# Windowed attention and a gated feed-forward layer: the product with w_in rewritten as seven block products, with chunks of 512 tokens

## The chip, the cores and the metric

One core of one Trainium2 chip runs the whole program. The metric is the device time of one execution in microseconds (us); lower is better. The core has five engines that run side by side and wait for each other through semaphores: TensorE (PE, matrix products into PSUM), VectorE (DVE), ScalarE (ACT), GpSimd (POOL) and SyncE (SP, which issues DMAs). Operands lie on chip in SBUF; products land in PSUM, of which the kernel uses eight banks of 128 x 512 float32.

## What is computed

```python
# q, k, v: (8 batches, 8 heads, 576 tokens, 64), float32; q and k are scaled by 8
scores = q @ k.T / 8 + slope[h] * -(i - j)            # ALiBi bias, slope[h] = 2 ** -(h + 1)
scores = where((i - j >= 0) & (i - j < 128), scores, -1e9)
attn = softmax(scores)
x = (attn @ v) as (4608 tokens, 512)                   # heads side by side
h = x @ w_in                                           # w_in: 512 x 2048, w_out: 2048 x 512
g = where(h >= 1, h, where(h <= -1, 0, (h + 1) ** 2 / 4))
out = g @ w_out                                        # 4608 x 512, float32
```

The two weight matrices arrive as 64-bit floats and are converted on the chip.

## The kernel before, in words

The 4608 tokens (the 8 batches behind each other) are cut into 12 chunks of `CH` = 384 tokens, three blocks of 128. Attention looks back 128 tokens, so a block of queries needs its own block of keys and the one in front: a window of 256 keys.

**Precision.** The kernel gives TensorE float32 operands in two forms: as plain float32 (48 written products of L396 stand as 96 instructions in the trace), called the slow form here, or as `F32R` (one instruction each), the fast form. For the fast form a value is split into a high part `a0` (a cast to F32R) and a low part `a1 = a - a0`, and a product is three fast products: `a0 b0 + a0 b1 + a1 b0`. The first `LIGHT` = 2 chunks of attention and the second layer of chunk 0 use the slow form instead, and need no splits.

**Attention**, for each head `m` (8 per chunk): `scores` makes the three windows' products (L246, or L248 and L249), adds the distance table `rel` and takes the row maximum (L252, DVE, 256 wide), exponentiates with a row sum (L254, ACT), and folds the two halves of the window into one 128-wide block while it divides by the sum (L267, DVE). `weights_t` transposes (L276, PE), splits (L286, L287) and cuts the block into the two triangles (L289, L291, POOL). `values` multiplies by v (L317 or L341) and adds up the parts (L342, L343, L345). `prepare_q`, `prepare_k`, `prepare_v` make splits of q, k, v.

**Feed-forward.** `split_x` splits the 512 x 384 block of x (L359, L360). `layer1(c, fc)` makes 128 of the 2048 features for the chunk: 12 products of 384 columns into the single PSUM bank of `ps_h` (L366 to L368), then the nonlinearity in three operations (L375 ACT, L376 and L377 DVE), and the split of g (L384 ACT, L385 POOL). `layer2(c, fc)` adds these features' share of the output into three accumulator banks: 9 products of 512 columns (L399 to L401; L396 in chunk 0). After the last one, L404 scales by 4 and a DMA stores. All split weights stay in SBUF through the run.

**Weights.** `fetch_weights` loads 64-bit pieces, issued on ACT's queue; `float32_of` converts (L115, L116 on ACT; L117, L118, L119 on DVE); `convert_in`, `convert_out` and `split_out` place them and split them (L138, L139, L151, L152).

**Order.** The kernel hands the instructions over in the order of the two interleaved lists at its end: `layer1` of piece i, `layer2` of piece i - `LAG`, and after each some segments of the next chunk's attention, so that attention of chunk c + 1 lies beside the feed-forward of chunk c. A list scheduler with a simulated timeline may move instructions within an engine; the order on each engine is then fixed in the program. PSUM: three accumulators, one bank for h, four for attention (`ps_a`).

Of the kernel before, what the change touches and what calls it, by code (L numbers as in the profile page):

```python
# [14 lines left out]
PSUM = bass.MemoryType.PSUM  # L15


@with_exitstack
def windowed_attention_then_ffn(
# [9 lines left out]

# [5 lines left out]
    DFF = w_in.shape[1]  # L45
# [3 lines left out]
    NFC = DFF // P  # L49
    NQB = 3  # L50
    CH = NQB * P
    NCHUNK = NT // CH
    NP = NCHUNK * NPAIR
    NH = 2 * NP
    CYCLE = 2 * SEQ // CH
    CUT = SEQ - CH
    assert 2 * SEQ == CYCLE * CH and CYCLE == 3 and CUT == P + D
    NEG = -1.0e30

# [3 lines left out]
    wp = ctx.enter_context(tc.tile_pool(name="wp", bufs=1))  # L63
    stg = ctx.enter_context(tc.tile_pool(name="stg", bufs=3))
    ap1 = ctx.enter_context(tc.tile_pool(name="ap1", bufs=1))
    xp1 = ctx.enter_context(tc.tile_pool(name="xp1", bufs=1))
    gp = ctx.enter_context(tc.tile_pool(name="gp", bufs=3))
    ps_acc = ctx.enter_context(tc.tile_pool(name="ps_acc", bufs=NQB, space=PSUM))
    ps_h = ctx.enter_context(tc.tile_pool(name="ps_h", bufs=1, space=PSUM))
    ps_a = ctx.enter_context(tc.tile_pool(name="ps_a", bufs=4, space=PSUM))  # L70

    def bank(name):
        return ps_a.tile([P, 4 * P], F32, name=name, tag="ps_a")

# [3 lines left out]
    quarter = const.tile([P, 1], F32, name="quarter")  # L78
    G.memset(quarter, 0.25)

    loaded = const.tile([P, 1], F32, name="loaded")
    S.activation(loaded, quarter, AF.Exp)
    qscale = const.tile([P, NPAIR], F32, name="qscale")
    for g in range(NPAIR):
        G.memset(qscale[:D, g:g + 1], 4.0 ** g / 4.0)
        G.memset(qscale[D:, g:g + 1], 4.0 ** g / 2.0)

    rel = const.tile([P, 2 * P], F32, name="rel")
    reli = stg.tile([P, 2 * P], I32, name="reli", tag="stg")
    G.iota(reli, pattern=[[1, 2 * P]], base=-P, channel_multiplier=-1)  # L90
    V.tensor_copy(rel, reli)
    G.affine_select(out=rel, in_=rel, pattern=[[1, 2 * P]], base=0, channel_multiplier=-1,
                    compare_op=ALU.is_gt, fill=NEG)
    G.affine_select(out=rel, in_=rel, pattern=[[-1, 2 * P]], base=P, channel_multiplier=1,
                    compare_op=ALU.is_ge, fill=NEG)
# [12 lines left out]

    def float32_of(w, name, out=None):

        low, high = w[..., 0], w[..., 1]
        f = stg.tile([P] + list(w.shape[1:-1]), F32, name=f"f_{name}", tag="stg")
        fi = f.bitcast(I32)

        S.mul(high.bitcast(F32), high.bitcast(F32), 2.0 ** -112)  # L115
        S.activation(low, low.bitcast(U32), AF.Copy, scale=2.0 ** -29)  # L116
        V.tensor_scalar(fi, high, 3, None, ALU.logical_shift_left)  # L117
        V.scalar_tensor_tensor(fi, high, -0x80000000, fi, ALU.bitwise_and, ALU.bitwise_or)  # L118
        V.tensor_tensor(fi if out is None else out.bitcast(I32), fi, low, ALU.add)  # L119
        return f  # L120

    raw = {}

    def fetch_weights(fc):
        w1 = wp.tile([P, NCC, P, 2], I32, name=f"rawi{fc}", tag=f"wi{fc}")
        S.dma_start(w1, wi32[:, 2 * fc * P:2 * (fc + 1) * P].rearrange("(c p) (f w) -> p c f w", p=P, w=2))

        if fc + 1 < NFC:
            w2 = wp.tile([P, DM, 2], I32, name=f"rawo{fc}", tag=f"wo{(fc + 2) % NFC}")
        else:  # L130
            w2 = ap1.tile([P, DM, 2], I32, name=f"rawo{fc}", tag="kl")
        S.dma_start(w2, wo32[fc * P:(fc + 1) * P, :].rearrange("p (f w) -> p f w", w=2))
        raw[fc] = (w1, w2)

    def convert_in(fc):
        f = float32_of(raw[fc][0], f"i{fc}")
        t = wi[fc] = wp.tile([P, 2, NCC, P], F32R, name=f"wi{fc}", tag=f"wi{fc}")
        S.copy(t[:, 0], f)  # L138
        V.tensor_tensor(t[:, 1], f, t[:, 0].bitcast(F32), ALU.subtract)  # L139
# [403 lines left out]
```

## Time and profile before

| what | value |
|---|---|
| times of three executions | 1068.0, 1070.49, 1070.89 us (median 1070.49) |
| profiled execution: span from its first to its last instruction | 1068.8 us |
| share of the span in which PE, DVE, ACT, POOL were busy | 97%, 76%, 58%, 35% |
| TensorE clock granted, mean | 0.980 of full |
| moved between HBM and chip | 69.51 MB |

The profiled execution has no separate time of its own beside the span: 1068.8 us lies inside the three runs' times and 1.7 us under their median. In the profile a line such as `L366 PE MATMUL h<-xh,wi 128*128 128x384 f32 x768` names the kernel line, the engine, the operation, output and inputs by tile name, the shapes, and the count; after it stand the busy time in us, the mean duration of one in ns, the engine's idle time ahead of them and what ended it. A matmul's duration includes its way through the array, so matmuls in a row start closer together than they last.

### The profile page before, as it was taken

To read this page: it belongs to the slowest core of one execution; us is meant where nothing else is said; L and a number is where in the kernel's file an instruction comes from. 1 tells how busy PE (TensorE), PEld (TensorE's weight loads), DVE (VectorE), ACT (ScalarE), POOL (GpSimd) and SP (SyncE) were. 2 spreads that over 40 slices of the span, in tenths; PEclk is the share of its full clock that TensorE was granted. 3 is DMA by queue.
4 is the path that set the end of the run, shared out by engine and by line. 5 is a ranking of instruction groups with operands and counts; after the bars stand their busy time and mean duration, and the time that the engine had idled before them with its cause. 6 is when DMAs were issued, how large, how long until landed. Compare 5 with 4: busy or idle time off the path is not lost.

```text
span 1068.8 us, 16893 instructions
## 1 busy us (share of the span) xinstructions
PE 1041.4 (97%) x5510; PEld 905.7 (85%) x5510; DVE 808.7 (76%) x2281; ACT 619.0 (58%) x1476; POOL 375.6 (35%) x419
## 2 busy tenths in 40 slices
PE   7999999999999999999999999999999999999998
PEld 5566668998999988998988998899899889899996
DVE  3889999879778788779887788877787897863322
ACT  4687767557557556557565555655565655742322
POOL 1121104343443343344443343344334444333221
PEclk7599999999999999999999999999999999999999
DMA  5466412212113112212221311311121221200000
GB/s 179 141 199 198 148 38 67 60 30 82 43 48 94 38 38 78 59 31 70 55 50 43 86 37 47 91 30 38 60 65 38 77 65 40 75 1 1 31 1 29
DMA packets 58904, 69.51 MB, mean 65 GB/s; under 512 B 4032, under 2 KB 44480, under 8 KB 58816
## 3 DMA queue, kind: packets, MB, share of 16 engines
q1 hardware_dynamic: 48064, 51.66, 17.2%
q10 hardware_dynamic: 10752, 16.78, 4.6%
q8 instruction: 43, 0.70, 0.3%
q14 instruction: 45, 0.37, 0.1%
HBM read 58.98 MB, written 9.44 MB: 64 GB/s over the span
## 4 chain that ended last, share of the span: by engine, by line
PE 83%; DVE 7%; ACT 4%; issue 2%; POOL 2%; DMA 1%; ACTq 0%; DVEq 0%; POOLq 0%
PE h L367 11%; PE h L366 11%; PE h L368 11%; PE acc L399 10%; PE acc L400 10%; PE acc L401 10%; PE x L341 5%; PE p L276 3%; PE acc L396 3%; PE x L317 2%; PE s L249 2%; PE s L248 2%; PE s L246 2%; ACT z L254 1%; DVE g L376 1%
## 5 line engine op out<-in xcount | busy, mean ns | idle before, releaser
L385 POOL TENSOR_TENSOR gl<-g,gh 128x384 fp32r<-128x384 f32 x176 | 183.3, 1041 | 414.5 <-ACT gh L384 403.4
L366 PE MATMUL h<-xh,wi 128*128 128x384 f32 x768 | 266.4, 347 | 3.3 <-ACT xh L359 2.8
L367 PE MATMUL h<-xl,wi 128*128 128x384 f32 x768 | 260.7, 339 | 0.4 <-DVE xl L360 0.4
L368 PE MATMUL h<-xh,wi 128*128 128x384 f32 x768 | 259.8, 338 | 0.0
L399 PE MATMUL acc<-wo,gh 128*128 128x512 f32 x528 | 211.8, 401 | 5.7 <-ACT gh L384 5.7
L376 DVE SCALAR_TENSOR_TENSOR g<-sg 128x384 f32<-128x384 f32 x192 | 108.4, 565 | 138.9 <-ACT sg L375 124.5
L400 PE MATMUL acc<-wo,gh 128*128 128x512 f32 x528 | 208.2, 394 | 0.0
L384 ACT CAST gh<-g 128x384 fp32r<-128x384 f32 x176 | 90.3, 513 | 187.8 <-DVE g L377 176.4
L375 ACT ACTIVATE sg<-h,quarter 128x384 f32<-128x384 f32 x192 | 111.1, 579 | 143.1 <-PE h L368 136.7
L401 PE MATMUL acc<-wo,gl 128*128 128x512 f32 x528 | 155.9, 397 | 0.2 <-POOL gl L385 0.2
L366 PEld LDWEIGHTS h<-xh,wi 128*128 128x128 f32 x768 | 144.6, 188 | 13.0 <-ACT xh L359 3.5
L254 ACT ACTIVATE z<-z,nmax 128x256 f32<-128x256 f32 (+2 forms) x288 | 139.1, 485 | 26.3 <-DVE nmax L252 23.2
L367 PEld LDWEIGHTS h<-xl,wi 128*128 128x128 f32 x768 | 144.6, 188 | 8.4 <-issue 2.7
L368 PEld LDWEIGHTS h<-xh,wi 128*128 128x128 f32 x768 | 144.6, 188 | 0.0
L267 DVE CUSTOM_DVE_ANT_0 ep<-z,rc 128x128 f32<-128x128 f32 x256 | 129.8, 548 | 1.3
L252 DVE CUSTOM_DVE_ANT_0 z<-s,rel 128x256 f32<-128x256 f32 (+2 forms) x256 | 94.0, 393 | 41.3 <-PE s L249 36.1
L289 POOL TENSOR_SCALAR_AFFINE_SELECT lu<-lu 128x768 fp32r<-128x768 f32 x80 | 80.7, 1008 | 121.6 <-DVE lu L287 114.1
L399 PEld LDWEIGHTS acc<-wo,gh 128*128 128x128 f32 x528 | 99.4, 188 | 24.8 <-ACT gh L384 8.0
L401 PEld LDWEIGHTS acc<-wo,gl 128*128 128x128 f32 x528 | 97.2, 188 | 19.9 <-POOL gl L385 0.4
L377 DVE SCALAR_TENSOR_TENSOR g<-sg,g 128x384 f32<-128x384 f32 x192 | 111.2, 579 | 3.3
L400 PEld LDWEIGHTS acc<-wo,gh 128*128 128x128 f32 x528 | 99.4, 188 | 16.4
L291 POOL TENSOR_SCALAR_AFFINE_SELECT lu<-lu 128x768 fp32r<-128x768 f32 x80 | 82.6, 1032 | 4.5
(83 smaller groups left out, 1491.5 us busy)
## 6 DMA issues: line engine op xcount, KB each, us to landing
kr<-in_k_dram SPq DMA_DIRECT2D x60, 256.0 KB, 4.1
qr<-in_q_dram SPq DMA_DIRECT2D x48, 192.0 KB, 3.4
out_dram<-o SPq DMA_DIRECT2D x36, 256.0 KB, 3.0
rawi<-in_moe_w_in_dram ACTq DMA_DIRECT2D x16, 512.0 KB, 3.9
rawo<-in_moe_w_out_dram ACTq DMA_DIRECT2D x16, 512.0 KB, 4.8
vn<-in_v_dram SPq DMA_DIRECT2D x32, 256.0 KB, 2.8
kr<-in_k_dram SPq DMA_DIRECT2D x28, 192.0 KB, 3.4
vn<-in_v_dram SPq DMA_DIRECT2D x16, 192.0 KB, 2.5
```

The lines of the kernel that those rows point to most:

```text
L254: S.activation(z[:, i, c0:], z[:, i, c0:], AF.Exp, bias=nmax[:, i:i + 1], scale=-1.0, accum_out=sm[:, i, 0:1])
L267: st["folded"] = V.tensor_tensor_reduce(out=ep[:, i, :], in0=z[:, i, :P], in1=z[:, i, P:], op0=ALU.add, op1=ALU.add, scale=rc[:, i:i + 1], ...
L366: T.matmul(ph, wi[fc][:, 0, cc, :], xh, start=(cc == 0), stop=False)
L367: T.matmul(ph, wi[fc][:, 0, cc, :], xl, start=False, stop=False)
L368: T.matmul(ph, wi[fc][:, 1, cc, :], xh, start=False, stop=(cc == NCC - 1))
L375: first = S.activation(sg, ph, AF.Relu, bias=quarter[:, 0:1], scale=0.25)
L376: V.scalar_tensor_tensor(g, sg, 0.5, sg, ALU.min, ALU.mult)
L377: last = V.scalar_tensor_tensor(g, sg, -0.25, g, ALU.add, ALU.max)
L385: G.tensor_tensor(gl, g, gh.bitcast(F32), ALU.subtract)
L399: T.matmul(a, gh[:, ts], wo[fc][:, 0], start=first, stop=False)
L400: T.matmul(a, gh[:, ts], wo[fc][:, 1], start=False, stop=False)
L401: T.matmul(a, gl[:, ts], wo[fc][:, 0], start=False, stop=last)
```

## The change

The kernel is rewritten around Strassen's algorithm (in Winograd's form) for `x @ w_in`. Chunks now have 2, then eight times 4, then 2 blocks of 128 tokens (`SIZES`): 256, 8 x 512, 256 tokens.

For a chunk of 512 tokens the features are taken in eight groups `g` of 2 x 128 (piece `g` and piece `8 + g`). The weights of a group form a 2 x 2 block matrix (two features pieces x two halves of the 512 inputs), the transposed x another (two halves of inputs x two halves of the tokens). Instead of 8 block products, 7 are made from sums of blocks; each has 6 fast products of 256 columns. Four of the seven accumulate one after another in one PSUM bank (`hA`), with the running sum copied out by ACT after the first three; three use the bank `hB`. DVE adds the copies to form the four blocks of h.

```diff
+PRODUCTS = (("A11", "B11"), ("A12", "B21"), ("S2", "T2"), ("S1", "T1"), ("S4", "B22"), ("S3", "T3"), ("A22", "T4"))
...
+    SIZES = [2] + [4] * 8 + [2]
...
+    def product(o, w, x, start, stop):
+        todo = [(kb, a, b) for kb in range(2) for a, b in ((0, 0), (0, 1), (1, 0))]
+        for n, (kb, a, b) in enumerate(todo):
+            T.matmul(o, w[:, a, kb], x[:, b, kb], start=start and n == 0, stop=stop and n == len(todo) - 1,
+                     skip_group_check=True)
...
+                def prod(n, st=st, g=g):
+                    w, x = PRODUCTS[n]
+                    o = st["A" if n in (0, 2, 3, 4) else "B"]
+                    product(o, use(c, g, w), xs[c, x], start=n in (0, 1, 5), stop=True)
+                    if n in (0, 2, 3):
+                        s = st[n] = fp.tile([P, 2 * P], F32, name=f"s{n}_{c}_{g}", tag=f"s{n}", bufs=1)
+                        S.copy(s, o)
+                    f1, f2 = st["h"]
+                    if n == 1:
+                        V.tensor_tensor(f1[:, :2 * P], o, st[0], ALU.add)
+                    if n == 4:
+                        S.copy(f1[:, 2 * P:], o)
+                        nonlinear(c, g, f1, 4 * P)
+                    if n == 5:
+                        V.tensor_tensor(f2[:, 2 * P:], o, st[3], ALU.add)
+                    if n == 6:
+                        V.tensor_tensor(f2[:, :2 * P], o, st[2], ALU.add)
+                        nonlinear(c, NG + g, f2, 4 * P)
+                    used(c, g, w)
...
+                for n, fill in ((2, 1), (3, 2), (4, 1), (5, 1), (6, 2)):
+                    steps.append([lambda prod=prod, n=n: prod(n), lambda tokens=tokens, n=n: tokens(n)])
+                    steps += [[f] for f in later(fill)]
```

A "fill" is one block of `layer2` (three products of 512 columns for one token block); the fills of a group are those of the group before it. Between product 0 and product 2 lie product 1 and one fill.

The weight operands (`A11`, `A12`, `A22`, and sums `S1` to `S4`) are no longer kept in SBUF. In chunk 1 `build` makes them (the sums on POOL, a cast on ACT, a subtraction on DVE) and stores each split operand, 256 KB, to a scratch in HBM; from chunk 2 on `fetch` streams each one back ahead of every use, ten operands ahead, through a ring of ten buffers. The last chunk uses the plain four blocks. Chunk 0 now makes its first layer in the slow float32 form with unsplit weights.

```diff
+    def build(g, name):
+        f = operand(g, name)
         t = ring.tile([P, 2, 2, P], F32R, name=f"b_{g}_{name}", tag="w")
         S.copy(t[:, 0], f)
         V.tensor_tensor(t[:, 1], f, t[:, 0].bitcast(F32), ALU.subtract)
+        d = scratch[g, name] = dr.tile([P, 4 * P], F32, name=f"d_{g}_{name}", tag=f"d_{g}_{name}")
+        DMA.dma_start(d, t.bitcast(F32).rearrange("p s c f -> p (s c f)"))
+    def fetch(c, g, name):
+        t = ring.tile([P, 2, 2, P], F32R, name=f"w_{c}_{g}_{name}", tag="w")
+        DMA.dma_start(t.bitcast(F32).rearrange("p s c f -> p (s c f)"), scratch[g, name])
+        return t
```

x is combined and split into seven operands instead of four (`combine`, `split_x`: four subtractions more on DVE, three casts and subtractions more).

The nonlinearity becomes clamp, square, maximum, and the factor 4 of the output goes away:

```diff
-        first = S.activation(sg, ph, AF.Relu, bias=quarter[:, 0:1], scale=0.25)
-        V.scalar_tensor_tensor(g, sg, 0.5, sg, ALU.min, ALU.mult)
-        last = V.scalar_tensor_tensor(g, sg, -0.25, g, ALU.add, ALU.max)
+        V.tensor_scalar(m, h, 1.0, -1.0, ALU.min, ALU.max)
+        S.activation(m, m, AF.Square, bias=half[:, 0:1], scale=0.5)
+        V.tensor_tensor(f, h, m, ALU.max)
```

In `scores` each query has exactly 128 keys in its window of 256, one of each pair (j, j + 128). A predicated copy now folds the two halves in PSUM right after the product, so all that follows is 128 wide, and the division by the row sum moves to ACT:

```diff
+        V.copy_predicated(pt[:, :nk, P:], older.unsqueeze(1).broadcast_to([P, nk, P]), pt[:, :nk, :P])
+            V.tensor_tensor_reduce(out=z[:, i], in0=pt[:, n, P:], in1=distances(b0 + i), op0=ALU.add, op1=ALU.min,
+                                   scale=-slope, scalar=3.0e38, accum_out=nmax[:, i:i + 1])
+            S.activation(z[:, i], z[:, i], AF.Exp, bias=nmax[:, i:i + 1], scale=-1.0, accum_out=sm[:, i:i + 1])
...
+                for i in range(nb):
+                    S.activation(z[:, i], z[:, i], AF.Copy, scale=rc[:, i:i + 1])
```

The light chunks' scores use all 128 rows, with zeros in the other head's rows of q. The conversion of the 64-bit weights takes two DVE operations instead of three (the sign comes from a parametric ReLU on ACT), reads through six 512 KB buffers, and its loads are issued on SP's queue together with all others. PSUM: four accumulators, the two banks hA and hB, and two banks for attention instead of four. The host lays v and both weight matrices out so that a load is contiguous.

More of the change, by code (lines that the diff above doesn't have):

```diff
@@ L48, in windowed_attention_then_ffn @@
     NCC = DM // P
[L49 to L57, printed above, removed]
+    NFC = 16
+    NG = NFC // 2
+    SIZES = [2] + [4] * 8 + [2]
+    STARTS = [sum(SIZES[:i]) for i in range(len(SIZES))]
+    NCHUNK = len(SIZES)
+    NH = NCHUNK * H
+    PERIOD = 2 * SEQ // P
+    assert sum(SIZES) * P == NT and 2 * SEQ == PERIOD * P
     NEG = -1.0e30
@@ L122, in windowed_attention_then_ffn @@
[L122 to L133, printed above, removed]
@@ L181, in load_v @@
+        for rows in lo_rows:
+            DMA.dma_start(kr[rows, :, :n + P],
+                          k[g * P:(g + 1) * P, t0 - P:t0 + n].rearrange("(j d) t -> d j t", j=2))
     def load_v(p):
         c, g = divmod(p, NPAIR)
-        nb = NQB + before(c)
+        nb, b0 = SIZES[c], STARTS[c]
+        if c == 0:
+            if g % 2 == 0:
+                t = pair[p]["v2"] = ring.tile([P, 2, nb, P], F32, name=f"vn_{p}", tag="w")
+            else:
+                t = pair[p - 1]["v2"]
+            pair[p]["vn"] = t[:, g % 2]
+            DMA.dma_start(t[:, g % 2], v[g, :, :nb])
+            return
@@ L225, in scores @@
         c = p // NPAIR
-        ql, kr, kk, kl = (pair[p].get(x) for x in ("ql", "kr", "kk", "kl"))
+        nb, b0 = SIZES[c], STARTS[c]
+        st = pair[p]
         if m not in head:
-            head[m] = dict(ep=ap1.tile([P, NQB, P], F32, name=f"ep_{m}", tag="ep", bufs=2),
-                           z=ap1.tile([P, NQB, 2 * P], F32, name=f"z_{m}", tag="z"),
-                           nmax=ap1.tile([P, 4], F32, name=f"nmax_{m}", tag="nmax", bufs=2),
-                           sum=sums[:, m % 2])
@@ L342, in values @@
-        S.copy(o, px[D:, :])
-        V.tensor_tensor(o, px[:D, :], o, ALU.add)
-        o = o[:, q0 * P:(q0 + 1) * P]
-        V.tensor_tensor(o, pf[:D, NQB, :], o, ALU.add)
+        nb = SIZES[c]
+        n = nb * P
+        lu = head[m]["lu"]
+        if c not in xn:
+            if c == 0:
+                xn[c] = xp.tile([P, NCC, n], F32, name=f"xn_{c}", tag="T4")
+            else:
+                xn[c] = xp.tile([P, NCC, 4 * P], F32, name=f"xn_{c}", tag="xn")
+        px = bank(c, f"x_{m}")[:, :n]
@@ new lines, in layer2 @@
+    def layer2(c, n, fc, t):
+        first, last = n == 0, n == NFC - 1
+        if first and t == 0:
+            accs[c] = [ps_acc.tile([P, DM], F32, name=f"acc_{c}_{i}", tag=f"acc{i // 2}") for i in range(SIZES[c])]
+        a = accs[c][t]
+        ts = slice(t * P, (t + 1) * P)
+        w = w_of[fc]
+        if c == 0:
+            T.matmul(a, gs[c, fc][:, ts], w[:, 1], start=first, stop=last)
+        else:
+            gh, gl = gs[c, fc]
+            T.matmul(a, gh[:, ts], w[:, 0], start=first, stop=False)
+            T.matmul(a, gh[:, ts], w[:, 1], start=False, stop=False)
+            T.matmul(a, gl[:, ts], w[:, 0], start=False, stop=last)
+        if last:
+            o = fp.tile([P, DM], F32, name=f"o_{c}_{t}", tag="o")
+            (V.tensor_copy if t % 2 else S.copy)(o, a)
+            r = (STARTS[c] + t) * P
+            DMA.dma_start(out[r:r + P, :], o)
+        if t == SIZES[c] - 1:
+            del gs[c, fc]
@@ L503, in windowed_attention_then_ffn @@
[L503 to L512 removed]
+                T.transpose(idle[:, i % 4 * P:(i % 4 + 1) * P], ident, ident)
+    for p in range(NPAIR):
+        load_qk(p)
+        if p % 2 == 0:
+            load_v(p)
+            pair_v = p
+        else:
+            load_v(p)
@@ L515 @@
+    for f in pending:
+        f()
 _INS = ["q", "k", "v", "moe_w_in", "moe_w_out"]
```

694 lines of the change are left out of this document (386 added, 308 removed).

## The prediction

> **What bounds the kernel now.** I read the page's busy shares first, then stretches (us of the span; length; busy us and instruction count of PE, PEld, DVE, ACT, POOL; granted clock; DMA share; GB/s).
>
> ```profile
> span 1068.8 us, 16893 instructions
> PE 1041.4 (97%) x5510; PEld 905.7 (85%) x5510; DVE 808.7 (76%) x2281; ACT 619.0 (58%) x1476; POOL 375.6 (35%) x419
> ...
> 0.00:32.00 32.00, 25.90 (x100) 17.12 (x100) 14.77 (x67) 15.63 (x42) 6.08 (x25) 0.69 0.62 201
> 32.00:70.00 38.00, 34.50 (x119) 20.69 (x119) 28.65 (x111) 26.14 (x72) 8.49 (x16) 0.72 0.43 138
> 70.00:120.00 50.00, 49.78 (x201) 32.25 (x200) 48.35 (x133) 36.62 (x82) 9.87 (x14) 1.00 0.59 193
> 120.00:161.00 41.00, 41.00 (x170) 27.72 (x169) 38.58 (x96) 27.98 (x58) 3.89 (x5) 1.00 0.22 69
> 161.00:245.00 84.00, 83.80 (x469) 75.41 (x468) 72.40 (x199) 54.31 (x131) 33.81 (x32) 1.00 0.18 51
> ...
> 244.90:328.50 83.60, 82.61 (x465) 75.17 (x464) 68.65 (x196) 51.17 (x125) 33.40 (x37) 1.00 0.23 63
> ...
> 993.80:1068.80 75.00, 69.80 (x346) 62.32 (x344) 18.17 (x33) 21.09 (x39) 17.21 (x17) 0.99 0.06 22
> ```
>
> The stretch 244.9 to 328.5 is one chunk of 384 tokens, from its first L366 to the next chunk's. PE is busy for 82.6 of 83.6 us, DVE for 82%, ACT for 61%: PE sets the pace. The first 161 us, for chunk 0 and two chunks of attention, are different: DVE is nearly full from 70 to 120, DMA runs at 138 to 201 GB/s up to 120, and the clock is 0.7 up to 70.
>
> What a product really takes is its step along the chain of waits, not its duration (start, us):
>
> ```profile
> 573.03 0.17 PE h L366
> 573.21 0.18 PE h L367
> 573.38 0.17 PE h L368
> 573.56 0.82 PE x L341 x7
> 574.38 0.33 PE p L276 x3
> ...
> 511.47 0.69 PE acc L401 x3
> ...
> 89.50 1.88 PE L396 MATMUL acc<-wf,g 128*128 128x512 f32 x4
> ...
> L396 PE MATMUL acc<-wf,g 128*128 128x512 f32 x90 | 41.7, 599 | 0.0
> L399 PE MATMUL acc<-wo,gh 128*128 128x512 f32 x528 | 211.8, 401 | 5.7 <-ACT gh L384 5.7
> ```
>
> Fast: 0.176 for 384 columns, 0.117 for 256 (the seven of L341, with shorter ones among them), 0.11 for 128, 0.231 for 512. Slow: 1.88 is three steps and one duration of 0.60, so 0.43 a step, two per written product: 0.86 for 512, 0.43 for 256. A present chunk is then 192 x 0.176 + 144 x 0.231 + 8 x (6 x 0.117 + 3 x 0.11 + 0.82) = 81.9, and took 83.6: 1.02 times its steps.
>
> **The change on PE.** A chunk of 512: the first layer has 8 groups x 7 products x 6 = 336 at 0.117 = 39.3 (before, scaled by 4/3: 45.1). Second layer 192 x 0.231 = 44.4, scores 64 x 0.117 = 7.5, transposes 32 x 0.11 = 3.5, values 0.82 x 8 x 4/3 = 8.7: the same work as before. Sum 103.4, against 109.2 for 512 tokens before. So seven-of-eight is worth 5.8 us a chunk, 46 over eight, if PE is fed as well as now.
>
> **The other engines in a chunk of 512.** Group means (ns) that the change moves:
>
> ```profile
> L376 DVE SCALAR_TENSOR_TENSOR g<-sg 128x384 f32<-128x384 f32 x192 | 108.4, 565 | 138.9 <-ACT sg L375 124.5 <-POOL gl L385 11.6 <-POOL lu L291 1.9
> L377 DVE SCALAR_TENSOR_TENSOR g<-sg,g 128x384 f32<-128x384 f32 x192 | 111.2, 579 | 3.3
> L267 DVE CUSTOM_DVE_ANT_0 ep<-z,rc 128x128 f32<-128x128 f32 x256 | 129.8, 548 | 1.3
> L267 DVE CUSTOM_DVE_ANT_0 ep<-z,rc x256: 330/349/1170, 13.2 to 956.8; 128x128 f32<-128x128 f32 x128
> L252 DVE CUSTOM_DVE_ANT_0 z<-s,rel 128x256 f32<-128x256 f32 x192 | 75.9, 419 | 28.8 <-PE s L249 26.9 <-PE s L246 1.1
> L252 DVE CUSTOM_DVE_ANT_0 z<-s,rel 128x128 f32<-128x128 f32 x32 | 9.2, 287 | 12.2 <-PE s L249 9.1 <-PE s L246 2.6
> L139 DVE TENSOR_TENSOR wi<-f_i,wi 128x512 fp32r<-128x512 f32 x16 | 10.9, 680 | 0.8 <-ACT wi L138 0.8
> L117 DVE TENSOR_SCALAR f_i<-rawi 128x512 int32<-128x512 int32 x16 | 7.3, 455 | 1.1 <-ACT rawi L115 1.1
> L118 DVE SCALAR_TENSOR_TENSOR f_i<-rawi,f_i 128x512 int32<-128x512 int32 x16 | 10.9, 681 | 0.1
> L375 ACT ACTIVATE sg<-h,quarter 128x384 f32<-128x384 f32 x192 | 111.1, 579 | 143.1 <-PE h L368 136.7 <-issue 2.2 <-ACT xn L324 1.0
> L138 ACT CAST wi<-f_i 128x512 fp32r<-128x512 f32 x16 | 9.8, 614 | 3.7 <-DVE f_i L119 2.8 <-DVE rc L267 0.5 <-DVE rc L261 0.2
> L254 ACT ACTIVATE z<-z,nmax 128x256 f32<-128x256 f32 x224 | 112.2, 502 | 13.2 <-DVE nmax L252 11.0 <-DVE g L376 0.9
> L254 ACT ACTIVATE z<-z,nmax 128x128 f32<-128x128 f32 x32 | 12.9, 403 | 13.1 <-DVE nmax L252 12.2 <-ACT lu L279 0.6
> L286 ACT CAST lu<-p 128x384 fp32r<-128x384 f32 x80 | 38.1, 477 | 12.4 <-PE p L276 11.3
> L82 ACT ACT_TABLE_LOAD x1 | 1.3, 1283 | 0.8 <-PEq L524 0.8
> ...
> 7.50 0.42 DVE L252 CUSTOM_DVE_ANT_0 z<-s,rel 128x256 f32<-128x256 f32 x1
> ...
> 7.85 0.42 DVE L252 CUSTOM_DVE_ANT_0 z<-s,rel 128x256 f32<-128x256 f32 x1
> ```
>
> DVE now has 68.65 x 4/3 = 91.5 per 512 tokens. The nonlinearity goes from 21.3 x 1.144 = 24.4 to 16 x (0.455 + 0.680) = 18.2. L267 goes: 32 x 0.548 = -17.5. L252 becomes 128 wide: 32 x 0.132 = -4.2. The predicated copies (16, priced as the 256-wide L252 that also reads PSUM): +6.7. Three additions per group out of PSUM, same price: 24 x 0.42 = +10. Splits and sums of x: 11 x 0.68 (L139) for 5.3 shorter ones (0.55: L139 less 0.13 for 128 columns, the step between L252's two rows): +4.5. Together -6.7; DVE 85, or 80% of 106.
>
> ACT now has 51.17 x 4/3 = 68.2. Exponentials lose 32 x 0.1 = -3.2, the nonlinearity and its cast, 16 of 512 for 21.3 of 384 (0.1 for each 128 columns, by L254's two rows), -2.5. Division by the sum is new: 32 x 0.40 = +12.9. Four copies per group out of PSUM, 256 wide: L286 less 0.1, so 32 x 0.37 = +11.8. Casts of x, 7 x 0.61 (L138) for 5.3 x 0.51: +1.6. Sum 89, or 84% of 106. POOL keeps its work (33.4 x 4/3 = 44 of 106). All remain below PE, so I keep the 46 us, less what tighter coupling costs.
>
> That coupling: product 3 adds to the bank that ACT must first have copied. With an idle ACT this is the way through the array (L399's 0.40 duration less its 0.23 step: 0.17), a hand-over, the copy 0.37 and a hand-over (0.04 each, row below).
>
> ```profile
> 1061.17 0.52 ACT gh L384
> 1061.69 0.04 issue
> 1061.73 0.50 PE acc L399
> ```
>
> That makes 0.62. It is covered by one fill, 0.69, and by attention's 19.7 us spread over some 64 blocks, 0.3 each. A busy ACT adds about half an operation times its share, 0.2. So cover exceeds need by 0.2 on average and fails sometimes. The other waits of a group (ACT's copies after products 0 and 3, DVE's reads after 1 and 5) have one or two blocks more, or the same one fill. Bounds are zero and, with all five late by 0.2, 8 us a chunk. I take 1%, nearest to the present row (1.02): 1.03 x 103.4 = 106.5 a chunk.
>
> **Streamed weights.** 56 operands x 256 KB = 14.7 MB a chunk. The present weights' queue, and the 256 KB stores:
>
> ```profile
> q10 hardware_dynamic: 10752, 16.78, 4.6%
> out_dram<-o SPq DMA_DIRECT2D x36, 256.0 KB, 3.0
> ```
>
> 16.78 MB took 4.6% of 1069 = 49 us of all engines, so 14.7 MB take 43 of 106, and DMA share goes from 0.23 to about 0.64. An operand has some nine products, 17 us, to land; 256 KB take 3. SP's queue holds everything now: an operand behind a q load that waits for its buffer waits too, for a few us of those 17. Cost taken: 0; if that cover is gone, a product waits 3 us.
>
> **The start.** Up to the first sweep of 512, PE steps are: attention of 256 tokens 13.9, first layer 64 x 0.43 = 27.5, second 32 x 0.86 = 27.5, attention of 512 tokens in slow form 31: 100. The weights (16.8 MB) and q, k, v of 768 tokens (4.7) at the 201 GB/s of the first stretch need 107; with the last pieces' products 112 is the lower bound. The upper is the present 161. DVE, which was full there, gets less: 32 conversions lose L118, 22 us, and the folds of L267 go. The loads move from ACT's queue to SP's, behind twelve loads of q, k, v that the first head needs first in either kernel. Twenty-two of the 38 warming transposes go; PE is not what ends this stretch, so I cost them at 0, and at full price they only bring the clock of 0.7 that the 32 to 70 row has anyway. I take 122, nearer to the loads.
>
> Chunk 1 makes operands: 64 builds and 16 splits, 80 x 0.68 on DVE = 54, 80 x 0.61 = 49 on ACT. Operations in a row overlap (the two L252 above last 0.42 and start 0.35 apart), so I count nine tenths: DVE 85 + 49 = 134, ACT 89 + 44 = 133. POOL's 32 sums, at 0.68 to twice that, leave it at 66 to 88. Chunk 1 is bound by DVE and ACT, not by PE's 103. Bounds: 107 (builds slip into idle time ahead) and 150 (nothing overlaps, and a tenth is waits). I take 134. The scratch stores wait for a split and stand in SP's queue ahead of loads of q and k that are due a pair of heads later: 0.
>
> **Sum.** 122 + 134 + 6 x 106.5 + chunk 8 with half the attention (93.6 x 1.03 = 96) + the last 256 tokens (192 x 0.117 + 96 x 0.231 = 44.7, and 8 as the present last chunk has beyond its 67 us of steps) 53 = 1044 of span, against 1068.8. By 768 tokens it is 256 against the present 245: the start gives back 11 of the gain. The median of the runs stood 1.7 above the span: 1045 to 1046; I say 1045.
>
> [...] L267, with two SBUF inputs, has a median of 349 and a mean of 548, with a maximum of 1170: some run three times as long. [...]
>
> **The rivals.** *The bank's chain decides (slower).* If ACT, at 84%, serves each of five waits 0.2 us later than covered, the list order fixed beforehand cannot absorb it: 1 us x 64 groups = 64, so 1045 + 64 - 8 (my 1%) = 1101. It decides from 0.4 us a group beyond my 1%, which eats the 25. For it: ACT's work grows by a third and attention's banks halve. Against: present PE waits are 1.2% with DVE at 82%. *Start and builds run long (slower).* 135 and 150: 1045 + 29 = 1074. *Everything is fed as now and builds slip into idle time:* start 112, chunk 1 at 115, factor 1.02: 1045 - 10 - 19 - 8 = 1008 to, with half of that, 1026. *The change does not pay on PE:* if weights cannot load at 0.117 over long runs of 256 columns (rows show seven in a row), or operands land late, a step of 0.14 costs 336 x 0.023 x 8 = 62: 1107. *Tables:* if the square or the parametric ReLU needs another table than the exponential, each change of function costs L82's 1.28; two for each of some 150 nonlinearities make 380: 1430. Against it: Exp, Relu and Copy run on one load now. [...]
>
> **How the numbers follow.** Forecast 1026 to 1062: 0.57. Fed as now: 0.12. Bank's chain 0.17, of it a third between 1062 and 1085. Long start 0.08. No gain on PE 0.04, tables 0.02. A measurement here tells 0.3%, 3 us, from no change: faster (below 1067) 0.71, same 0.07, slower 0.22. Range 1012 to 1090 leaves out half of the slow chain, no gain on PE, the tables and a sliver below, 0.18 in all. The forecast's own range is 1026 to 1062.
>
> **What would show it.** Right: product steps of 0.117 in the first layer; about 106 us between chunks with PE over 97% busy; chunk 1 near 134 with DVE over 90%; first sweep of 512 starting near 122. Wrong: PE waiting for ACT's copies of the bank by more than 0.4 us a group, operands late by DMA, or ACT over 90%.

## The result: slower by 6.7%

After the change the kernel takes 1141.25 us (median of five runs, 1140.0 to 1146.27), before 1070.27 in the same comparison: a ratio of 1.067, 95% interval 1.065 to 1.070. 1045 was predicted, 1012 to 1090 the range. The profiled execution, the slowest of the five, has a span of 1144.2 us, 100 more than the 1044 of the sum. From its page:

```profile
span 1144.2 us, 19669 instructions
PE 1046.4 (91%) x6320; PEld 919.0 (80%) x6320; DVE 802.8 (70%) x1934; ACT 744.7 (65%) x1894; POOL 404.7 (35%) x370
```

PE's share falls from 97% to 91%, and it is not pushed aside by a fuller engine: DVE's share falls too, ACT's rises by 7 points to 65%. So no other engine has become the full one, and waits are the suspect. The stretches (us of the span; length; busy us and count of PE, PEld, DVE, ACT, POOL; clock; DMA share; GB/s) are cut where the products of a new chunk begin:

```profile
0.00:33.00 33.00, 17.71 (x67) 14.24 (x68) 22.40 (x65) 21.77 (x55) 11.00 (x30) 0.74 0.93 337
33.00:144.40 111.40, 99.28 (x405) 74.09 (x404) 77.18 (x242) 72.25 (x189) 19.51 (x29) 0.91 0.47 150
144.40:287.50 143.10, 120.59 (x722) 106.70 (x720) 128.26 (x281) 106.41 (x283) 65.56 (x55) 0.92 0.48 154
287.50:402.40 114.90, 110.31 (x705) 98.76 (x706) 81.36 (x200) 79.93 (x204) 42.78 (x32) 0.99 0.63 186
402.40:518.70 116.30, 109.60 (x710) 97.56 (x709) 85.96 (x200) 79.45 (x205) 45.64 (x32) 1.00 0.62 182
...
752.50:877.60 125.10, 114.93 (x705) 102.00 (x705) 88.28 (x201) 81.11 (x205) 41.14 (x32) 0.95 0.57 170
877.60:988.30 110.70, 105.00 (x692) 94.83 (x690) 80.34 (x184) 73.24 (x188) 43.41 (x34) 1.00 0.57 171
988.30:1088.50 100.20, 96.51 (x609) 86.08 (x607) 51.19 (x132) 52.97 (x131) 34.26 (x44) 1.00 0.56 167
1088.50:1144.20 55.70, 50.73 (x314) 45.38 (x312) 17.97 (x40) 18.66 (x39) 14.46 (x18) 0.98 0.44 142
```

Against the terms of the sum: the start 144.4 for 122 (+22); chunk 1 143.1 for 134 (+9); chunks 2 to 7 together 700.8 for 639 (+62); chunk 8 +4; the last 256 tokens +3. Some six tenths of the miss lie in the steady part, chunks 2 to 7.

What PE waited for in chunks 2 to 7 (total us, times, longest us), and for comparison the first two rows of the same view of the kernel before, over a stretch of 749 us (245 to 994):

```profile
PE hA L411 <- ACT s L539: 14.3, 16, 1.9
PE p L323 <- ACT z L314: 5.8, 6, 1.2
PE hB L411 <- DVE h L542: 5.1, 4, 2.0
PE acc L445 <- ACT gh L430: 5.1, 8, 1.1
PE hB L411 <- DVE h L547: 2.6, 4, 0.9
PE hA L411 <- ACT h L544: 1.9, 3, 1.1
```

```profile
PE x L341 <- POOL lu L291: 5.7, 7, 1.3
PE acc L399 <- ACT gh L384: 5.2, 5, 1.4
```

The wait for `gh` is as it was. New are the two product banks being emptied (L539 and L544 by ACT, L542 and L547 by DVE) and the transposes waiting for the division, now on ACT (L314). These views show only a part of the loss. Added up from the trace, as the distance from one product's start to the next one's less the step of its width, PE lost some 78 us in chunks 2 to 7, and some 20 in the 749 us before: about 21 at L539, 11 at L314, 9 at L430, 15 at the other three rows, some 11 in products at half clock, the rest in small pieces.

One copy of the bank in the timeline (start, length; idle time and its releaser in brackets; of the rows in this stretch, those of ACT and of PE's products into the two banks):

```profile
446.52 0.96 PE L411 MATMUL hA<-x_B,w_A 128*128 128x256 f32 x6
446.74 0.58 ACT L368 COPY xn<-x 64x512 f32<-64x512 f32 x1
447.31 0.87 PE L411 MATMUL hB<-x_B,w_A 128*128 128x256 f32 x6
447.35 0.73 ACT L270 CAST vs<-vn 128x640 fp32r<-128x640 f32 x1
448.10 0.59 ACT L326 CAST lu<-p 128x512 fp32r<-128x512 f32 x1
448.59 0.72 ACT L419 ACTIVATE m<-m,half 128x512 f32<-128x512 f32 x1
449.21 0.36 ACT L539 COPY s<-hA 128x256 f32<-128x256 f32 x1
449.46 0.63 ACT L430 CAST gh<-h 128x512 fp32r<-128x512 f32 x1
449.62 0.98 PE L411 MATMUL hA<-x_T,w_S 128*128 128x256 f32 x6 [0.68 <-ACT s L539]
```

The product into hA is done at about 447.5. ACT is in the middle of four operations of attention and of the previous group, each 0.58 to 0.73, and starts the copy 1.7 us later; PE stands idle for 0.68 before the next product into hA. ACT was never "full" here (79.5 of 116 us). It was in order, and the copy was the fifth in the line. Over the 144 such copies of chunks 2 to 7 the start lies 0.84 us behind the product's end in the mean and 2.25 at the ninetieth percentile, where 0.2 was assumed; the products in between cover 2.6 us in the mean, where 1.0 was assumed; 25 of the 144 still release the next product directly.

### The profile page after: what moved, and what is told of

It reads as the page before. It is cut to its first block, busy times and chain, and to the rows that moved or that the text cites. A ratio compares the mean times of both kernels' runs of the same rounds, so it can differ in the third digit from the quotient of the medians.

```text
span 1144.2 us, 19669 instructions
## 1 busy us (share of the span) xinstructions
PE 1046.4 (91%) x6320; PEld 919.0 (80%) x6320; DVE 802.8 (70%) x1934; ACT 744.7 (65%) x1894; POOL 404.7 (35%) x370
## 4 chain that ended last, share of the span: by engine, by line
PE 67%; DVE 15%; ACT 10%; issue 4%; DMA 2%; POOL 1%; SPq 1%; DVEq 0%; ACTq 0%; POOLq 0%
PE hA L411 12%; PE acc L445 10%; PE acc L446 10%; PE acc L447 9%; PE hB L411 8%; PE x L363 5%; PE acc L442 2%; PE p L323 2%; PE h L596 2%; PE h L411 2%; PE s L299 2%; ACT m L419 2%; DVE ql L250 2%; PE s L300 2%; DVE h L424 1%
## 5 line engine op out<-in xcount | busy, mean ns | idle before, releaser
L431 POOL TENSOR_TENSOR gl<-h,gh 128x512 fp32r<-128x512 f32 x128 | 192.1, 1507 | 263.8 <-ACT gh L430 251.2
L336 POOL TENSOR_SCALAR_AFFINE_SELECT lu<-lu 128x1024 fp32r<-128x1024 f32 (+3 forms) x88 | 85.2, 968 | 379.6 <-DVE lu L328 248.3
L306 ACT ACTIVATE z<-z,nmax 128x128 f32<-128x128 f32 x288 | 113.5, 395 | 58.8 <-DVE nmax L304 57.7
L419 ACT ACTIVATE m<-m,half 128x512 f32<-128x512 f32 (+1 forms) x160 | 107.8, 679 | 56.7 <-DVE m L418 53.3
L424 DVE TENSOR_TENSOR h<-h,m 128x512 f32<-128x512 f32 x128 | 115.1, 903 | 14.5 <-ACT m L419 14.3
L411 PE MATMUL hA<-x_T,w_S 128*128 128x256 f32 x672 | 104.0, 289 | 14.3 <-ACT s L539 12.5
L411 PEld LDWEIGHTS hA<-x_T,w_S 128*128 128x128 f32 x672 | 91.9, 191 | 23.5 <-ACT s L539 16.9
L314 ACT ACTIVATE z<-z,rc 128x128 f32<-128x128 f32 x240 | 77.9, 392 | 50.3 <-DVE rc L309 49.7
L539 ACT COPY s<-hA 128x256 f32<-128x256 f32 x192 | 69.7, 363 | 48.0 <-PE hA L411 47.4
L430 ACT CAST gh<-h 128x512 fp32r<-128x512 f32 x128 | 79.2, 621 | 25.3 <-DVE h L424 25.0
L363 PEld LDWEIGHTS x<-lu,vs 128*128 128x128 f32 x608 | 83.7, 192 | 12.3 <-POOL lu L338 4.8
L363 PE MATMUL x<-lu,vs 128*128 128x128 f32 (+1 forms) x608 | 84.8, 275 | 6.4 <-POOL lu L338 3.9
L338 POOL TENSOR_SCALAR_AFFINE_SELECT lu<-lu 128x1024 fp32r<-128x1024 f32 (+3 forms) x88 | 88.2, 1002 | 4.9 <-DVE lu L328 1.1
```

The lines of the kernel that those rows point to most:

```text
L306: S.activation(z[:, i], z[:, i], AF.Exp, bias=nmax[:, i:i + 1], scale=-1.0, accum_out=sm[:, i:i + 1])
L336: G.affine_select(out=b.bitcast(kind), in_=a.bitcast(F32), pattern=[[0, n], [-1, P]], base=0, channel_multiplier=1, compare_op=ALU.is_gt, ...
L338: G.affine_select(out=a.bitcast(kind), in_=a.bitcast(F32), pattern=[[0, n], [1, P]], base=0, channel_multiplier=-1, compare_op=ALU.is_ge, ...
L363: T.matmul(px[:, q0 * P:q1 * P], st, mv.rearrange("p a w -> p (a w)"), start=(w == 0), stop=(w == len(todo) - 1), skip_group_check=True)
L411: T.matmul(o, w[:, a, kb], x[:, b, kb], start=start and n == 0, stop=stop and n == len(todo) - 1, skip_group_check=True)
L419: S.activation(m, m, AF.Square, bias=half[:, 0:1], scale=0.5)
```

## Experiments

Each ran against the kernel before on the same chip; ratios are to it. "The kernel after" at 1141 has ratio 1.067.

### The hand-over of the product banks

```diff
-                        S.copy(s, o)
+                        S.copy(s, rel.rearrange("p a b -> p (a b)")[:, :2 * P])
```

> The three copies of bank hA per group read a constant from SBUF instead of the bank, so ACT does the same number of copies but product 2, 3 and 4 no longer wait for ACT; the sums of h are therefore not those of the reference. Theory 1 (the bank's chain sets the loss): in the six chunks from 287 to 988 us PE lost 78 us beyond its steps, 21 of them waiting for these copies and about 11 at half clock; 25 to 35 us go, 1106 to 1116. Theory 2 (ACT's queue is late as a whole, and the bank only shows it): the waits come back at the transposes (now 11 us), at the cast of g (9) and at the bank's next group; under 12 us go, 1130 or more.

1118.09 us, ratio 1.044 (1.042 to 1.047): 23 less, between the two theories; chunks 2 to 7 took 685.5, only 15 less. Then, besides, the additions after products 1 and 5 were made to read the constant instead of bank hB:

```diff
-                        V.tensor_tensor(f1[:, :2 * P], o, st[0], ALU.add)
+                        V.tensor_tensor(f1[:, :2 * P], rel.rearrange("p a b -> p (a b)")[:, :2 * P], st[0], ALU.add)
```

> As the run before, and DVE's additions after products 1 and 5 read a constant instead of bank hB, so no product but the first of a group in each bank waits for a read of its bank (sums of h again not the reference's). Theory 1: another 11 us for hB go, 1095 to 1105. Theory 2: within 5 us of the run before.

1130.14, ratio 1.055 (1.052 to 1.058); chunks 2 to 7 704.8, no less than after's 700.8. The copies of hA were gone as a cause, and PE's loss was some 74 us all the same; it stood now elsewhere: 17 us at the split of x (L386) ahead of a product into hA, 10 at the transposes, some 24 in products at half clock. Its first two waits in chunks 2 to 7:

```profile
PE hA L411 <- DVE x_T L386: 13.8, 6, 2.9
PE p L323 <- ACT z L314: 8.1, 3, 4.2
```

That is outside both theories again: with more waits taken out the run is 12 us slower than the one before it, and why is not shown. Taking out the wait that the trace names first returned 15 us of these chunks in one run and nothing in the next.

The order of the products turned round, so that A and B alternate and each bank has longer between its uses:

```diff
+TURN = (0, 1, 2, 5, 3, 4, 6)
...
```

> Same work and result, only the order of the seven products: A, B, A, B, A, A, B with a fill between each two, so that a copy of bank hA has a product of the other bank and two fills to pass (2.1 us of PE instead of 0.7 to 1.4). Theory 1: most of the 33 us of waits at hA and hB in the six chunks go, and some of the half clock: 25 to 45 us, 1096 to 1116. Theory 2: the copies stay late by ACT's queue, but 2.1 us cover a median lateness of 0.5 to 1.2: 10 to 20 us, and waits rise at transposes and casts.

1142.96, ratio 1.068 (1.065 to 1.072): nothing, where either theory had some gain; the wait for the copies of hA stays at 26 us by the sum over the trace. With the division by the row sum back on DVE:

```diff
-            if c < LIGHT:
+            if True:
```

> The division by the row sum in chunks from 2 on goes back from ACT (four operations of 0.39 per head) to DVE (one of 512 columns, about 0.7): ACT loses 12.5 us a chunk, DVE gains 5.5. Theory 1: the chain is as before, copies a little earlier: 5 to 15 us go. Theory 2 (ACT's load and order make the lateness): 25 to 50 us go, since ACT falls from 69% to 59% of a chunk and the transposes no longer wait for it (11 us).

1134.33, ratio 1.060 (1.057 to 1.063): 7 us. And with the instructions in the order in which the program lists them, no scheduler moving them:

```diff
-    with tile.TileContext(nc, schedule_with_timeline_sim=True) as tc:
+    with tile.TileContext(nc, schedule_with_timeline_sim=False) as tc:
```

> The changed kernel without the simulated timeline in the scheduler, so the order on each engine is another one, made without that estimate of times. If the loss is in an order that a wrong estimate packed too closely: 1090 to 1130. If the load of the in-order engines makes it: no gain, 1140 or more (with every order).

1139.06, ratio 1.065 (1.063 to 1.068), chunks of 116.6 to 118.2, a loss of some 75 us. It is not one unlucky order. Nor is it the clock: chunks 2 to 7 of this run, and below it those of the run with copies and additions cut, take the same time at a granted clock of 1.00 and of 0.94.

```profile
275.70:978.10 702.40, 662.47 (x4222) 573.40 (x4221) 497.60 (x1178) 477.62 (x1200) 248.98 (x193) 1.00 0.61 177
267.40:972.20 704.80, 667.83 (x4252) 607.51 (x4251) 520.67 (x1211) 493.39 (x1233) 250.78 (x196) 0.94 0.61 178
```

### The banks of attention

The second theory: not the product banks, but that attention has two banks where it had four. The kernel before, with that alone:

```diff
-    ps_a = ctx.enter_context(tc.tile_pool(name="ps_a", bufs=4, space=PSUM))
+    ps_a = ctx.enter_context(tc.tile_pool(name="ps_a", bufs=2, space=PSUM))
```

> The kernel before with two PSUM banks for attention instead of four, nothing else. Theory 3 (attention's waits, moved through fewer banks, throw the fixed order of the engines out of step, whatever the products do): 30 to 60 us slower, 1100 to 1130, with waits at scores, transposes and casts. Theory 1 (Strassen's bank chain): within 10 us of the kernel before.

1141.69 us, ratio 1.066 (1.063 to 1.069): one number changed in the kernel before costs as much as the whole change, and more than the 30 to 60 expected. That the two totals agree is chance: here the start is as before (768 tokens on, at 243.7 for 244.9), and all of the loss lies in the chunks behind it. Its chunks of 384 go from 83.6 to about 90.3, or 8.9 us per 512 tokens, where the kernel after misses its forecast by 10.3 a chunk. Its first three waits between 300 and 990 us, by the same view as above:

```profile
PE s L248 <- DVE lu L287: 12.1, 8, 1.7
PE s L248 <- DVE xn L345: 5.6, 8, 0.9
PE h L366 <- ACT sg L375: 5.0, 8, 1.6
```

The scores of the next head (L248) wait until DVE has read the transposes of an earlier one out of its bank (L287). And it is spread: even the single bank of `ps_h` (L366 behind L375), which made PE wait once before (0.3 us), now does 8 times.

If that were all, giving the kernel after four banks would cure it. This run shares two accumulator banks between four blocks of tokens to make room:

```diff
-        if c < LIGHT and turn[0] % 2:
+        if turn[0] % 2:
             return ps_acc.tile([P, 4 * P], F32, name=name, tag="acc1")
...
-        a = accs[c][t]
+        a = accs[c][t % 2]
...
```

> The changed kernel with four PSUM banks for attention, as the kernel before has. The two banks come from the accumulators: the second layer of token blocks 2 and 3 adds into the banks of blocks 0 and 1, so it makes the same products but the output is not that of the reference. Theory 3 (the two banks for attention are what costs): a chunk of 512 falls from 117 to 106 to 109, as the kernel before with two banks lost 6.6 us per 384 tokens; with chunk 1 and 8 gaining too, 1060 to 1090. Theory 1 (the chain of the product banks): chunks of 113 or more, 1115 to 1141.

1158.98, ratio 1.083 (1.079 to 1.087), chunks 2 to 7 715.9, a loss of some 90 us: worse, and beyond both theories. Its waits are at the product banks (L539 13.4, L542 7.5, L549 6.2, L544 5.3 us); none is for a shared accumulator to be copied out. So neither shortage's removal alone brings the chunks back: with attention's alone left they took 704.8, with the product banks' alone 715.9. That leaves the theory that either is enough, and it was tested by both edits together (this last run's, and that in which the copies and additions read a constant; no other line differs):

> Four banks for attention (accumulators shared two by two) and both product banks free of reads in between: h and the output are not the reference's, the work is the same. Theory 5 (either shortage alone is enough to put PE out of step, so removing one shows nothing): chunks of 106 to 109, 1060 to 1090. Theory 2 (ACT and DVE, in-order and 70% busy, serve every hand-over late, whichever it is): waits move again, chunks stay at 113 or more, 1110 or more.

1074.68, ratio 1.004 (1.003 to 1.006). From its stretches:

```profile
0.00:145.00 145.00, 117.57 (x474) 88.76 (x474) 101.04 (x315) 97.05 (x254) 30.67 (x59) 0.87 0.57 192
145.00:276.80 131.80, 114.20 (x696) 100.48 (x695) 124.03 (x257) 97.41 (x260) 67.08 (x53) 0.95 0.51 168
276.80:390.20 113.40, 108.78 (x707) 98.27 (x706) 93.62 (x205) 83.84 (x208) 41.53 (x32) 0.97 0.63 185
390.20:496.90 106.70, 106.16 (x705) 96.35 (x705) 85.73 (x198) 80.10 (x202) 43.63 (x32) 1.00 0.67 195
496.90:603.90 107.00, 106.34 (x705) 96.38 (x704) 85.11 (x198) 80.15 (x202) 43.66 (x32) 1.00 0.66 195
...
817.20:923.00 105.80, 104.93 (x702) 95.79 (x701) 84.10 (x192) 77.73 (x195) 43.55 (x32) 1.00 0.62 187
```

From chunk 3 on a chunk takes 105.8 to 107.0 us with PE busy for more than 99% of it, where 106.5 was forecast. The loss over chunks 2 to 7 is some 20 us, as over the 749 us of the kernel before. So the seven products and the streamed operands cost what the prediction had for them, and DVE and ACT with the same work left PE fed; the two shortages of banks were not as it had them. That both kinds of bank count rests on the differences between these runs, not on the waits that a trace names: with the product banks' reads cut, PE waited for the split of x more than for attention's banks. The feed-forward was timed by itself, with attention left out from the fifth chunk on:

```diff
+        if c >= 4:
+            xn[c] = xn[3]
...
```

> Attention is left out from the fifth chunk on (x of the fourth is used again, so the output is not the reference's); the sweeps of chunks 3 to 8 are the feed-forward alone, 83.7 us of PE steps each. If the chain of products, copies and nonlinearity is too slow by itself: 90 or more a chunk. If it is attention's work in ACT's and DVE's queues that makes its hand-overs late: 84 to 87 a chunk. Six such sweeps: 1144 less some 190 to 210.

1002.05 us. The sweeps of chunks 3 to 7, without attention, take 90.9 to 91.3 us for 83.7 of steps: 7.4 more a chunk, 0.92 for each of eight groups. Not all of it is the product banks: over the five chunks PE waited 9.4 us for them (L541, L546 and L551 of this run's kernel, whose lines stand two further down) and 7.8 for the cast of g (L432). And without attention's products there is less to cover a hand-over.

### Suspects that were cleared

```diff
-            o = fp.tile([P, DM], F32, name=f"o_{c}_{t}", tag="o")
+            o = fp.tile([P, DM], F32, name=f"o_{c}_{t}", tag="o", bufs=3)
```

> Changed kernel with three buffers for output blocks instead of two, so that ACT's second copy out of an accumulator does not stand in its queue until a store has landed (2.05 us in the chain at 415.7, with the copies of bank hA queued behind). If that hold sets the loss at a chunk's start, 1 to 3 us a chunk go: 1120 to 1133. If it is hidden: within 4 us of 1141.

A third buffer for the output rows, since the chain of waits showed ACT's copy of them (L450) held by a store for 2.05 us: 1148.37, ratio 1.072 (1.069 to 1.076); no gain, rather a loss.

```diff
+        if c >= 3:
...
+            return held[0]
```

> From chunk 3 on all products read one operand that was loaded once: no streaming (h is therefore wrong), DMA share from 0.6 to about 0.2. If streamed operands or the traffic cost PE anything, more than 10 us go; by the trace no product waited for an operand's load, so within 5 us of 1141, as the prediction costed it (0).

No weights streamed from chunk 3 on: 1144.94, ratio 1.069 (1.065 to 1.072). The 14.7 MB a chunk cost nothing, as predicted.

```diff
-        S.mul(high.bitcast(F32), high.bitcast(F32), 2.0 ** -112)
+        S.activation(high.bitcast(F32), high.bitcast(F32), AF.Prelu, scale=2.0 ** -112, alpha=2.0 ** 32)
...
-        V.scalar_tensor_tensor(fi, high, -0x80000000, fi, ALU.bitwise_and, ALU.bitwise_or)
```

> The kernel before with one part of the change: the sign of the 64-bit weights from the parametric ReLU, so 32 operations of 0.68 less on DVE in the first 120 us. If DVE sets the start (97% busy from 70 to 120), the second chunk begins 5 to 20 us earlier: 1050 to 1065. If loads and slow products set it: within 3 us of 1070.

The new conversion in the kernel before: 1070.2, ratio 1.000 (0.998 to 1.003), though DVE was busy for 40.5 us instead of 48.4 from 70 to 120 us.

```diff
-        V.tensor_tensor(t[:, 1], f, t[:, 0].bitcast(F32), ALU.subtract)
+        G.memset(t[:, 1].bitcast(F32), 0.0)
```

> In chunk 1 the low halves of the 64 operands are set to zero on POOL instead of being subtracted on DVE (h loses accuracy): DVE loses 64 x 0.6 = 38 us of the 128 it is busy in the 143 of chunk 1. If chunk 1 is bound by DVE, as predicted, it falls to 110 to 120 and the time to 1115 to 1122; if by the chain of the banks or ACT, to 130 to 140 and the time stays over 1130.

1137.5, ratio 1.062 (1.059 to 1.065); chunk 1 took 134.5 instead of 143.1, with DVE busy for only 99 us of it instead of 128. DVE alone is not its bound. In the run with both shortages removed chunk 1 took 131.8 with all its builds; with the product banks' reads cut alone it took 130.6 and 123.0, and in the order as written, with both shortages, 134.9. These stretches do not hold the same products (661 to 722 of them), so which of the two takes the 9 us above the forecast's 134 stays open.

### The start

```diff
...
-                operands_upto(AHEAD)
+                with ExitStack() as stack:
+                    for ins in held_at:
+                        stack.enter_context(tc.issue_after(ins))
+                    operands_upto(AHEAD)
```

> The changed kernel with the first ten operands of chunk 1 held back behind the middle of chunk 0's feed-forward; in the trace ACT, DVE and POOL make them from 19 us on, among the first heads' attention and the conversions. If they delay the start, the first sweep of 512 begins at 130 instead of 144 and chunk 1 lengthens by part of it: 1130 to 1138. If the chain of a head and the conversions set the start: 142 to 146, and the time within 4 us of 1141.

The first ten operands of chunk 1 are built later: 1146.37, ratio 1.071 (1.067 to 1.074); the first sweep of 512 begins at 140.8 instead of 144.4, and the time is no shorter.

With 16 more warming transposes at each head of the first chunk:

```diff
+        keep_busy(16)
```

> The kernel after, with 16 more warming transposes per head in the first chunk, so that TensorE has no long idle stretch while it waits for the heads' conversions; nothing else differs. After, the first sweep of 512 rows begins at 144.4 us, and between 10 and 70 us TensorE is at a lower granted clock, with a head every 6.9 us, of which about 3.8 us is its own products at that clock. If that clock sets the start: the sweep begins at about 130, and the time is near 1128. If the heads' conversions and the builds on VectorE and ScalarE set it: it begins at 142 to 146, and the time is within 4 us of 1141. If the added transposes themselves stand in the way of the heads: later than 148.

1140.94, ratio 1.067 (1.064 to 1.070); the sweep begins at 149.9. The transposes were all moved ahead of 33 us and did not answer the question, so they were run with the order as written:

> The order as written, with 16 more warming transposes at each head of the first chunk. In the run as_written without them the first sweep of 512 rows began at 140.8 us, the time was 1139.1, and the granted clock from 10 to 70 us was 0.71 and 0.86. In the kernel after the same transposes had all been moved ahead of 33 us by the list scheduler, so that the clock from 33 to 70 stayed at 0.68, and the sweep began at 149.9; here they stay at their heads. If the clock in that stretch sets the start: the sweep begins at 125 to 132, and the time is below 1130. If the heads' chain through the other engines sets it: 138 to 146, within 5 us of 1139.

1139.61, ratio 1.062 (1.055 to 1.069); the sweep begins at 138.8, against 140.8 in the same order without them. Two stretches in the same order without the added transposes, then the same of this run:

```profile
33.00:70.00 37.00, 28.66 (x125) 21.47 (x123) 30.85 (x108) 31.10 (x85) 10.98 (x17) 0.86 0.69 248
70.00:140.80 70.80, 70.52 (x297) 51.15 (x296) 53.38 (x155) 46.21 (x120) 9.47 (x13) 1.00 0.48 152
```

```profile
33.00:70.00 37.00, 33.99 (x203) 28.21 (x202) 34.16 (x112) 34.57 (x93) 10.97 (x16) 1.00 0.85 290
70.00:140.00 70.00, 70.00 (x298) 50.91 (x298) 50.16 (x147) 42.70 (x111) 9.14 (x13) 1.00 0.42 131
```

The clock from 33 to 70 us went from 0.86 to 1.00, and 2 us came of it. (In the kernel after it is 0.72 there, but in another order.) From 33 to 70 us the heads of chunk 0 and the conversions nearly fill DVE and ACT (34.2 and 34.6 of 37 us in this run); from 70 on PE is full to the last, for 69 to 74 us. Whether those two engines' load or the latency of a head's way through all four engines holds the first 70 us was not separated further.

## Why the prediction was wrong

**PE's steps: right.** For 256 columns 0.117 was forecast and 0.120 measured, for 512 columns 0.231 and 0.23; with PE fed, a chunk took the forecast's 106.5.

**The coupling, 1%: the step that failed.** Its two halves:

- "A busy ACT adds about half an operation times its share, 0.2." That is the wait of a copy that arrives at random at an engine with a queue of one. Here ACT runs in an order fixed beforehand, and the copy stands behind whatever was put ahead of it, four operations in the case shown. Measured: 0.84 in the mean, 2.25 at the ninetieth percentile. The cover was underestimated as well (1.0 for a measured 2.6), so means still said "covered". What cost time was the tail.
- Attention's banks. That they halve stood in the rival as a remark, and in the sum at 0, with no reason given. In the kernel before this one edit costs 71 us.

The two overlap, so they may not be added: each by itself takes a chunk to some 114 to 119 (the runs with one of them removed), and with both removed a chunk takes 106.5 from the third on (the second 113.4). Why the costs saturate rather than add is not shown in detail; a stall at one bank gives the other engines the time in which they would have fallen behind at the other, which fits the waits moving about, and is argued only.

The rival *the bank's chain decides* was this mechanism, at 0.17. Its 1 us a group is near the 0.92 measured without attention, and the six chunks lost 1.29 a group beyond the forecast. It stopped at 1101 because the start's 22 us were not in it and because 1 us a group was too little, and was held unlikely because "present PE waits are 1.2%": a number of a kernel with twice the banks for attention.

**The start, 122: wrong, +22.** Its bound was taken from the loads at the 201 GB/s of the kernel before. The loads ran at 337 GB/s over the first 33 us and 272 from there to 70, so 201 was no ceiling. What failed is the step that let the loads set the start, with PE's 100 us beside them: PE's last 69 to 74 us come after a first part that DVE, ACT and the heads' chain take up to 70, and the two add. The relief of DVE by the new conversion, 22 us of its time, was no lever either: in the kernel before it gained nothing. Twenty-two warming transposes at 0 was right: more of them, at full clock, moved the start by 2 us.

With this start even a well fed PE would not have won, as far as the run with both shortages removed shows. There the sweeps of chunk 2 begin at 276.8, 32 us behind the 245 of the kernel before at the same token (11 were forecast), and all chunks after it win back 27.

**Chunk 1, +9:** the mechanism of DVE and ACT as its bound was half right: DVE is busy for 128 of the 143, but with 29 us less on DVE the chunk lost only 9. Waits for the banks are in it (L539 3.3, L547 2.3, L542 1.9, L549 1.2 us of PE's); that they make the whole excess is not shown.

**Right at 0:** streamed weights (no product waited for them in chunks 2 to 7) and the tables. The trace has one load in all, with squares and the parametric ReLU beside the exponential:

```profile
L90 ACT ACT_TABLE_LOAD x1 | 1.3, 1283 | 0.8 <-PEq L677 0.8
```

**Loads of DVE and ACT: 85 and 89 us a chunk forecast, 84 and 80 measured** (the first four of chunks 2 to 7). So "ACT over 90%" was the wrong sign to look for: ACT at 69% was late often enough. The maximum took longer than its price. Two groups, with their mean in ns behind the busy time, and the spread of their durations (ns, least, median, most):

```profile
L418 DVE TENSOR_SCALAR m<-h 128x512 f32<-128x512 f32 (+1 forms) x160 | 72.3, 458 | 78.6 <-ACT h L544 54.0
L424 DVE TENSOR_TENSOR h<-h,m 128x512 f32<-128x512 f32 x128 | 115.1, 903 | 14.5 <-ACT m L419 14.3
...
L418 DVE TENSOR_SCALAR m<-h x160: 386/425/1480, 66.1 to 1135.2; 128x512 f32<-128x512 f32 x128, 128x256 f32<-128x256 f32 x32
L424 DVE TENSOR_TENSOR h<-h,m x128: 660/692/1815, 172.7 to 1090.8; 128x512 f32<-128x512 f32 x128
```

The maximum, with two SBUF inputs, took 903 in the mean for the 680 of L139: 3.6 us a chunk that the sum lacked. The trace shows when it runs longer. Of its 128 executions, the 68 during which POOL ran nothing took 0.69 us, and the other 60 took 1.15 in the mean. Each of the 43 that took over 0.70 began while a POOL instruction ran, and ended 0.54 to 0.55 us after that one's end, as here:

```profile
449.69 1.09 POOL L336 TENSOR_SCALAR_AFFINE_SELECT lu<-lu 128x1024 fp32r<-128x1024 f32 x1 [8.62 <-DVE lu L328]
449.86 1.46 DVE L424 TENSOR_TENSOR h<-h,m 128x512 f32<-128x512 f32 x1
```

That the POOL instruction is what holds it up is read from this pattern of 0.69 and 1.15 us alone; no run was made for it. The clamp's mean, 458, is the 455 of L117, so it cost the sum nothing, but a like pattern shows in it: with POOL idle it took 0.42, and seven of the 128 of 512 columns took 0.86 to 1.48 and ended 0.28 us after the POOL instruction that ran when they began.

## What to carry to other kernels

Count PSUM banks as a term of the sum, not as a remark: for each stage, how many banks it has before and after, and what the distance from one use to the next covers; a kernel whose attention had half its banks lost 6.6% here with no arithmetic changed. Size a hand-over by the longest run of operations that may stand ahead of it on an engine whose order is fixed beforehand (1.7 us in the case shown), not by that engine's busy share (79.5 of 116 us there). When several small waits share the blame, remove them together before you clear one: removed alone they returned 23 or 11 of the 71 us, or cost 18 more. No version that does the whole work beats the kernel before.

## What the runs showed that was not expected

Short waits were followed by a lower clock. In the kernel after, PE waits 0.49, 0.51 and 1.11 us within 3 us, and the products after them start 0.43 apart instead of 0.23:

```profile
754.58 0.39 PE L299 MATMUL s<-kk,ql 128*128 128x256 f32 x1 [0.49 <-DVE lu L328]
...
755.82 0.39 PE L411 MATMUL hA<-x_T,w_S 128*128 128x256 f32 x1 [0.51 <-ACT x_T L385]
757.32 0.80 PE L445 MATMUL acc<-wo,gh 128*128 128x512 f32 x1 [1.11 <-ACT gh L430]
757.91 0.63 PE L446 MATMUL acc<-wo,gh 128*128 128x512 f32 x1
758.34 0.63 PE L445 MATMUL acc<-wo,gh 128*128 128x512 f32 x1
```

The granted clock is 1.00 up to 756.6, when the third wait is not yet over, and about half from there on:

```profile
753.20:756.60 3.40, 2.01 (x13) 1.41 (x11) 3.40 (x6) 2.44 (x5) 1.94 (x2) 1.00 0.67 210
756.60:757.30 0.70, 0.00 (x0) 0.00 (x0) 0.70 (x2) 0.62 (x1) 0.70 (x1) 0.50 0.00 0
757.30:763.50 6.20, 6.18 (x18) 5.13 (x19) 5.46 (x11) 2.70 (x7) 3.64 (x3) 0.51 0.03 4
```

PE was busy for 2.0 of the 3.4 us ahead of the drop. The waits were followed by 6.2 us at half speed, 3 more lost, in which PE counts as busy; such stretches are part of why PE's busy time per chunk (105 to 115 us) exceeds its steps of 103. The clock's record changes in steps of 3.41 us in this run: its shortest entries last that long, and all but the last, which ends with the run, are whole multiples of it. In chunks 2 to 7 of this run it fell after eight such steps, in which PE was busy for 0.33 to 0.59 of the time, and after none with 0.63 or more. In chunk 1 it stayed up after two with 0.50 and 0.54, so this is what one run shows and no sharp limit. No single wait of PE in chunks 2 to 7 exceeds 2.0 us, so the clock fell without a longer one.
